# Sums of x in one run while GpSimd is held, sums of w_in moved, and chunk 4's transposes ahead of its v rows

## The chip, the cores and the metric

The kernel runs on one core of one Trainium2 chip. The metric is the device time of one execution in microseconds (us); lower is better. A core has five engines that run side by side, each in its own program order: TensorE (PE) multiplies matrices into PSUM, VectorE (DVE) and ScalarE (ACT) work elementwise on PSUM and SBUF, GpSimd (POOL) works elementwise on SBUF, and SyncE (SP) here only issues DMA transfers. They wait for each other on semaphores, which the framework places from the data dependences. The order of the instructions on each engine is the order in which the program calls them: there is no scheduler that changes it.

## The reference

Two layers follow each other. The first is a recurrent attention ("retention") over 768 steps, for 4 batches, 8 heads and a head size of 64:

```
gamma = 1.0 - 2.0 ** (-5.0 - arange(8));  scale = 1 / sqrt(64)
for t in range(768):
    state = gamma * state + outer(k[t], v[t])      # one 64 x 64 state for each batch and head
    y[t]  = scale * (q[t] @ state)
x = y, reordered to (3072 tokens, 512)
```

The second is a feed-forward layer: `h = x @ w_in` (512 to 2048), `g = gelu_tanh(h)`, `out = g @ w_out` (2048 to 512). Inputs and output are float32; the kernel computes in float16 with float32 sums.

## The kernel before

The sequence is cut into 6 chunks of 128 steps; a chunk has 4 batches, so 512 tokens. For each chunk c and batch b the kernel loads the rows of q, k and v, scales and casts them to float16, transposes q and k (by a DMA from chunk 2 on), forms the 128 x 128 scores of a head (`a_ps`, masked on DVE into `a_sb`), adds what the state contributes (`y_ps`), writes the result scaled by `dec` into `xT[c]`, and updates the state `st`.

The matrix products of the feed-forward layer go by quadrants with 7 block products in place of 8 (Winograd's form of Strassen's method). That needs sums of quadrants of both factors: `s_g` of g and `t_w` of w_out for the second product of every chunk, and `s_x` of x and `t_in` of w_in for the first product of chunks 3, 4 and 5 (the first product of chunks 0 to 2 is a plain one, `moe1` and `moe1_two`). The sums of x and w_in run on DVE, the sums of g mostly on POOL.

```python
s_x = const.tile([128, 4, 2, 2, 128], F16, name="s_x")

def tt(eng, out, in0, in1, op):
    eng.tensor_tensor(out=out, in0=in0, in1=in1, op=op)      # "L393" in the profile

def win_sums(i):          # 4 DVE sums of 128x512 float16 for one quarter of w_in
    ...
    tt(nc.vector, t[1], q[0, 1], q[1, 1], ALU.add)
    tt(nc.vector, t[2], t[1], q[0, 0], ALU.subtract)
    tt(nc.vector, t[3], q[0, 0], q[0, 1], ALU.subtract)
    tt(nc.vector, t[4], q[1, 0], t[2], ALU.subtract)

def x_sums(c, *keys):     # up to 4 DVE sums of 128x512 float16
    ...
    for j, in0, in1 in ops:
        if j in keys:
            tt(nc.vector, t[j], in0, in1, ALU.subtract)

def att_S(c, *bs):        # state update: products on PE (mm_s), 8 small instructions on DVE (ev_S)
    mm_s(c, bs)
    ev_S(c, bs)

def att_AY(c, bs, tag, ca, abs_, eng):   # outputs of chunk c, batches bs; scores of chunk ca, batches abs_
    for b in bs:   mm_yc(c, b, tag)
    for b in abs_: mm_A(ca, b)
    for b in bs:   mm_yi(c, b)
    if tag == "o":
        for b in abs_: ev_A(ca, b)
    for b in bs:   ev_Y(c, b, eng)
    if tag != "o":
        for b in abs_: ev_A(ca, b)

def prep_kT(c, b):        # cast of k on ACT, then the DMA transpose of q and k, issued from SP
    prep1(AC, "k", c, b)
    dma_T(c, b)

def run(units, after):    # unit i of the feed-forward layer on PE, then what is listed under i
    for i, u in enumerate(units):
        u()
        for f, *args in after.get(i, ()):
            f(*args)
```

The kernel is a row of such runs. The first runs the second product of chunk 0 (`units_0`, 15 units); the next the first product of chunk 1 (`moe1_two`, 16 units), then the second product of chunk 1 (`units_w(1)`, 14 units), the first product of chunk 2 (`moe1(2, fc)`, 16 units). The lists beside them are in the diff. From there on, `step(c)` for c = 2, 3, 4 mixes the second product of chunk c (units `u[0]` to `u[13]`), the first product of chunk n = c+1 (`h`, with the seven products `h.mm(0..6)`) and the attention of chunk m = c+2:

```python
for i in range(2):
    G = (2 * i, 2 * i + 1)
    for g in G:
        h.mm(0, g); h.keep(AC, 0, g)     # keep: ACT copies a PSUM bank to SBUF
        h.mm(1, g); h.add(1, g)          # add: DVE adds a PSUM bank to such a copy, which frees the bank
    h.act(1, *G)                         # act: gelu on ACT
    if i == 0: u[0](); u[1](); A(m, 0)   # A: scores on PE, masked on DVE
    else:      u[7](); u[8](); A(m, 2); sums(n, 0, 1, 2)    # sums: sums of g on POOL
    for g in G:
        h.mm(2, g); h.keep(AC, 2, g)
        h.mm(3, g); h.keep(AC, 3, g)     # mm(3) takes a bank that add(1) freed
    ...
    h.mm(4, *G); h.add(4, *G); h.act(4, *G)
    if i == 1:
        u[11](); sums(n, 0, 4); Y(m, 3)  # u[11] ends in a store of output rows, issued from POOL
    h.mm(5, *G); h.add(5, *G)
    if i == 0: u[4](); Y(m, 1); u[5](); St(m, 0, 1)
    elif m < NCk: x_sums(m, 1, 2); u[12]()
    h.mm(6, *G)
    ...
    if i == 0: u[6]()
    else:
        u[13](); St(m, 2, 3)
        if m < NCk: x_sums(m, 3, 4)
```

Of the kernel before, what the change touches and what calls it, by code (L numbers as in the profile page):

```python
# [16 lines left out]
def kernel(  # L17
# [417 lines left out]
    t_in = {}  # L435
    s_x = const.tile([128, 4, 2, 2, 128], F16, name="s_x")

# [16 lines left out]

    def x_sums(c, *keys):
        t = {j: s_x[:, j - 1] for j in (1, 2, 3, 4)}
        w = {(K, x): x_blk(c, K, x) for K in range(2) for x in range(2)}
        ops = (
            (1, w[0, 1], w[0, 0]),
            (2, w[1, 1], t[1]),  # L460
            (3, w[1, 1], w[0, 1]),
            (4, w[1, 0], t[2]),
        )
        for j, in0, in1 in ops:
            if j in keys:
                tt(nc.vector, t[j], in0, in1, ALU.subtract)

# [90 lines left out]
    class Half:  # L558
# [10 lines left out]
        def rhs(self, key, k):  # L569
            if key in s_g:  # L570
                return s_x[:, key - 1, k]
            return x_blk(self.c, *key)[:, k]
# [260 lines left out]
    def rows_of(c):  # L833
        for b in range(B):
# [14 lines left out]
            11: [(mm_Y, 0, "h"), (att_T, 2, AC), (ev_Y, 1, 0)],  # L849
            12: [(mm_Y, 1, "att"), (ev_Y, 1, 1), (mm_s, 1, (0,))],  # L850
            13: [(att_1A, 2), (ev_S, 1, (0,))],
            14: [(att_S, 1, 1)],
        },
# [9 lines left out]
        {  # L863
            0: [(att_T, 3)],
            1: [(mm_Y, 2, "o"), (ev_Y, 1, 2)],
            2: [(att_1A, 3)],
            3: [(att_S, 1, 2), (g_sums, PO, 1, 0, 4, 0, 1)],
            4: [(prep1, AC, "q", 2, 0)],
            5: [(mm_Y, 3, "o"), (ev_Y, 1, 3), (prep_kT, 2, 0)],
            6: [(att_S, 1, 3), (prep1, AC, "q", 2, 1)],  # L870
            7: [(g_sums, PO, 1, 4, 8, 0, 1), (prep_kT, 2, 1)],
# [3 lines left out]
            11: [(g_sums, PO, 1, 0, 4, 1, 2), (prep_kT, 2, 3), (rows_of, 3)],  # L875
            13: [(win_sums, 0)],
            14: [(att_AY, 1, (), "o", 2, (0, 1), None), (prep1, PO, "v", 2, 0), (prep1, PO, "v", 2, 1)],
# [6 lines left out]
            4: [(att_AY, 2, (0, 1), "h", 2, (2, 3), AC)],  # L884
            1: [(win_sums, 1)],
            6: [(prep_qk, 3, 0)],
            7: [(att_S, 2, 0, 1), (prep_qk, 3, 1)],
            9: [(att_AY, 2, (2, 3), "h", 2, (), AC), (att_S, 2, 2, 3), (prep_qk, 3, 2)],
            10: [(prep1, PO, "v", 3, b) for b in range(B)],
            11: [(prep_qk, 3, 3), (rows_of, 4)],  # L890
            13: [(win_sums, 2)],
        },
# [3 lines left out]
    def sums(c, f, *keys, eng=PO):  # L896
        for f0 in range(f, f + 4, 2):
# [5 lines left out]
            0: [(win_sums, 3)],  # L903
            2: [(att_AY, 3, (), "att", 3, (0, 1), None)],
            3: [(g_sums, PO, 2, 0, 2)],
            6: [(att_AY, 3, (0, 1), "o", 3, (2, 3), VE)],
            7: [(g_sums, PO, 2, 2, 4), (prep1, PO, "v", 4, 0), (prep1, PO, "v", 4, 1)],
            8: [(att_S, 3, 0, 1), (prep_qk, 4, 0)],
            11: [(g_sums, PO, 2, 4, 6), (prep_qk, 4, 1), (rows, 5, 0), (rows, 5, 1)],
            12: [(att_AY, 3, (2, 3), "o", 3, (), VE), (att_S, 3, 2, 3)],  # L910
            14: [(x_sums, 3, 1, 2, 3, 4)],
            15: [(g_sums, PO, 2, 6, 8), (prep1, PO, "v", 4, 2), (prep1, PO, "v", 4, 3)],
        },
# [26 lines left out]
    def step(c):  # L940
# [8 lines left out]
        for i in range(2):  # L949
# [44 lines left out]
            if i == 1:  # L994
                u[11]()
                sums(n, 0, 4)
                Y(m, 3)
            h.mm(5, *G)
# [6 lines left out]
            elif m < NCk:  # L1005
                x_sums(m, 1, 2)
                u[12]()
# [8 lines left out]
            if i == 0:  # L1016
                u[6]()
            else:
                u[13]()
                St(m, 2, 3)  # L1020
                if m < NCk:
                    x_sums(m, 3, 4)

# [40 lines left out]
```

## Time and profile before

| | us |
|---|---|
| time, median of 3 runs | 211.17 (210.99 to 212.71) |
| span of the profiled execution | 207.6 |
| PE busy | 193.7 (93% of the span) |
| DVE busy | 148.9 (72%) |
| POOL busy | 133.5 (64%) |
| ACT busy | 117.8 (57%) |

The span is the time from the first to the last instruction in the trace of one execution. "Busy" is the time in which an engine had an instruction under way. Lines such as L393 name the line of the program that issued an instruction; because `tt` is a helper, all sums have the line L393, and the tile they write tells them apart: `s_x` and `t_in` (DVE), `s_g` (POOL), `h_sb` and `o_sb` (DVE additions of a PSUM bank). L581 is a matrix product of `h.mm`, L499 one of `u[...]`, L350 one of the plain first product, L208 the scores, L267 and L286 the state update on PE and DVE, L198 the DMA transpose, L86 a load of rows. Some rows of the table of groups (busy us, mean ns of one, then the idle time before them and what ended most of it):

```profile
L221 DVE TENSOR_TENSOR a_sb<-a_ps,mask 128x512 f16<-128x512 f32 x48 | 30.5, 683 | 10.2 <-PE a_ps L208 8.1
L393 DVE TENSOR_TENSOR h_sb<-h_ps,h_sb 128x512 f32<-128x512 f32 x36 | 22.9, 683 | 7.9 <-ACT h_sb L143 7.2
L286 DVE SCALAR_TENSOR_TENSOR st<-st,cst,s_ps 64x128 f16<-64x128 f16 (+1 forms) x80 | 20.6, 319 | 0.7 <-PE s_ps L267 0.5
```

Times within the span are given below as "at 139.9", in us from its start.

### The profile page before, as it was taken

The page shows a single profiled execution, that of the slowest core. Times are in us where ns is not written, and L with a number is a line of the kernel's source. Part 1 is how long each engine was busy: PE and PEld are TensorE (multiplying, and loading weights), DVE is VectorE, ACT ScalarE, POOL GpSimd, SP SyncE. Part 2 cuts the span into 40 slices and gives each one's busy share as a digit, 9 for nine tenths or more (in the row PEclk, how much of TensorE's full clock was granted, in tenths as well). Part 3 has the DMA queues.
Part 4 walks back from the last instruction along what each step waited for, and adds up shares of the span by engine and source line. Part 5 has one row for each costly group of instructions (what it writes and reads, how often), then busy time and mean ns, then how long its engine had stood idle before and what let it go on. Part 6 is the DMA issues. An engine that isn't in the chain of part 4 may idle for free.

```text
span 207.6 us, 5024 instructions
## 1 busy us (share of the span) xinstructions
PE 193.7 (93%) x2012; PEld 149.9 (72%) x2012; DVE 148.9 (72%) x295; ACT 117.8 (57%) x216; POOL 133.5 (64%) x132
## 2 busy tenths in 40 slices
PE   5798999999999989999979999994999999999993
PEld 1456747788687868654567888874788888888882
DVE  5346669679978999969796966998844883336720
ACT  2384564463399318356638697444876285876321
POOL 0599333952099999558399739479919479598200
PEclk9999999999999999999999999999999999999998
DMA  7999999999967998999999596520250031002204
GB/s 167 288 257 207 206 206 277 346 296 275 288 153 104 213 250 185 181 280 244 213 215 207 122 255 151 179 107 2 67 37 0 3 163 43 0 0 99 106 14 188
DMA packets 87094, 34.24 MB, mean 165 GB/s; under 512 B 80032, under 2 KB 84512, under 8 KB 87072
## 3 DMA queue, kind: packets, MB, share of 16 engines
q1 hardware_dynamic: 73920, 19.25, 43.7%
q0 software_dynamic: 6624, 12.58, 23.4%
q10 hardware_dynamic: 6528, 2.10, 4.0%
q8 instruction: 15, 0.25, 0.5%
q14 instruction: 7, 0.06, 0.1%
HBM read 27.63 MB, written 6.29 MB: 163 GB/s over the span
## 4 chain that ended last, share of the span: by engine, by line
PE 75%; DVE 12%; POOL 3%; DMA 3%; ACT 2%; SPq 2%; issue 1%; DVEq 0%; ACTq 0%
PE o_ps L499 27%; PE h_ps L350 17%; PE h_ps L581 15%; DVE s_x L393 5%; DVE st L286 4%; PE o_ps L619 3%; DMA k<-in_k_dram 3%; PE y_ps L243 3%; PE a_ps L208 3%; PE o_ps L652 2%; PE y_ps L230 2%; DVE h_sb L393 2%; POOL qk L159 2%; ACT g L370 1%; SPq L86 1%
## 5 line engine op out<-in xcount | busy, mean ns | idle before, releaser
L350 PE MATMUL h_ps<-xT,w_in 128*128 128x256 f16 (+2 forms) x296 | 45.6, 304 | 0.5 <-ACT g L370 0.5
L370 ACT ACTIVATE g<-h_ps 128x512 f16<-128x512 f32 (+1 forms) x54 | 31.1, 583 | 21.9 <-PE h_ps L350 20.2
L393 POOL TENSOR_TENSOR s_g<-g 128x512 f16<-128x512 f16 x30 | 35.3, 1185 | 12.6 <-ACT g L370 8.2
L221 DVE TENSOR_TENSOR a_sb<-a_ps,mask 128x512 f16<-128x512 f32 x48 | 30.5, 683 | 10.2 <-PE a_ps L208 8.1
L350 PEld LDWEIGHTS <-w_in 128*128 128x128 f16 x296 | 26.5, 98 | 15.2 <-issue 1.2
L370 ACT ACTIVATE g<-h_sb 128x512 f16<-128x512 f32 x36 | 21.8, 632 | 22.8 <-DVE h_sb L393 22.7
L499 PEld LDWEIGHTS <-s_g 128*128 128x128 f16 x320 | 30.7, 98 | 5.0 <-POOL s_g L393 1.0
L499 PE MATMUL o_ps<-t_w,s_g 128*128 128x256 f16 x240 | 29.4, 273 | 0.8 <-POOL s_g L393 0.8
L393 DVE TENSOR_TENSOR h_sb<-h_ps,h_sb 128x512 f32<-128x512 f32 x36 | 22.9, 683 | 7.9 <-ACT h_sb L143 7.2
L159 POOL TENSOR_TENSOR v<-v,cst 128x512 f16<-128x512 f32 x20 | 21.0, 1071 | 7.2 <-DMA v<-in_v_dram 4.5
L581 PEld LDWEIGHTS <-t_in 128*128 128x128 f16 x192 | 18.0, 98 | 6.4 <-issue 3.5
L499 PEld LDWEIGHTS <-g 128*128 128x128 f16 x208 | 20.2, 98 | 2.5
L393 POOL TENSOR_TENSOR s_g<-s_g,g 128x512 f16<-128x512 f16 x18 | 21.0, 1168 | 1.4
L286 DVE SCALAR_TENSOR_TENSOR st<-st,cst,s_ps 64x128 f16<-64x128 f16 (+1 forms) x80 | 20.6, 319 | 0.7 <-PE s_ps L267 0.5
L581 PE MATMUL h_ps<-s_x,t_in 128*128 128x256 f16 x144 | 18.1, 273 | 3.1 <-DVE h_sb L393 3.0
L393 POOL TENSOR_TENSOR s_g<-g,s_g 128x512 f16<-128x512 f16 x18 | 20.8, 1168 | 0.1
L143 ACT COPY h_sb<-h_ps 128x512 f32<-128x512 f32 x36 | 19.2, 599 | 1.5 <-PE h_ps L581 1.3
L499 PE MATMUL o_ps<-w_out,g 128*128 128x256 f16 x160 | 19.1, 273 | 0.0
L259 DVE TENSOR_TENSOR xT<-y_ps,dec 128x512 f16<-128x512 f32 x20 | 13.3, 683 | 4.1 <-PE y_ps L243 4.1
L581 PEld LDWEIGHTS <-w_in 128*128 128x128 f16 x144 | 13.9, 98 | 1.9
L143 ACT CAST qk<-q 128x512 f16<-128x512 f32 x20 | 12.6, 630 | 2.2 <-DMA q<-in_q_dram 2.2
L143 ACT CAST qk<-k 128x512 f16<-128x512 f32 x20 | 12.6, 631 | 0.1
(81 smaller groups left out, 279.0 us busy)
## 6 DMA issues: line engine op xcount, KB each, us to landing
out_dram<-o_sb POOLq DMA_DIRECT2D x10, 512.0 KB, 3.1
k<-in_k_dram SPq DMA_DIRECT2D x18, 256.0 KB, 4.6
q<-in_q_dram SPq DMA_DIRECT2D x18, 256.0 KB, 4.7
v<-in_v_dram SPq DMA_DIRECT2D x18, 256.0 KB, 4.7
w_in<-in_moe_w_in_dram POOLq DMA_DIRECT2D x4, 512.0 KB, 9.0
w_out<-in_moe_w_out_dram POOLq DMA_DIRECT2D x4, 512.0 KB, 14.1
q<-in_q_dram POOLq DMA_DIRECT2D x4, 256.0 KB, 11.2
k<-in_k_dram POOLq DMA_DIRECT2D x4, 256.0 KB, 9.5
```

The source lines that it names most:

```text
L143: eng.copy(out=out, in_=in_)
L159: eng.tensor_tensor(out=t, in0=src, in1=cst[:, col:col + H].unsqueeze(2).broadcast_to([128, H, Dh]), op=ALU.mult,)
L208: nc.tensor.matmul(out=ps[j][:, hp], lhsT=t[j * 64:(j + 1) * 64, 1, hp], rhs=t[j * 64:(j + 1) * 64, 0, hp], start=True, stop=True,)
L221: nc.vector.tensor_tensor(out=s, in0=ps[j], in1=mask[:, j], op=ALU.mult)
L243: nc.tensor.matmul(out=y_ps[j * 64:(j + 1) * 64, hp], lhsT=h16["v", c, b][:, 2 * hp + j], rhs=a_sb[c, b, j][:, hp], start=(c == 0), stop=True,
L259: nc.vector.tensor_tensor(out=x, in0=ps, in1=dec, op=ALU.mult)
L286: nc.vector.scalar_tensor_tensor(out=t[:, :, hp], in0=t[:, :, hp], scalar=cst[sl, OG + hp:OG + hp + 1], in1=s_ps[sl, :, hp], op0=ALU.mult, ...
L350: nc.tensor.matmul(out=out, lhsT=w_in_sb[wi][:, kc, wr * 128:(wr + 1) * 128], rhs=xT[c][:, kc, t0:t1], start=(kc == 0), stop=(kc == NHP - ...
L370: nc.scalar.activation(out=out, in_=in_, func=AF.Gelu_apprx_tanh, scale=1.0)
L393: eng.tensor_tensor(out=out, in0=in0, in1=in1, op=op)
L499: nc.tensor.matmul(out=po, lhsT=lhs(c, lk, fp, a), rhs=rhs(rk, fp), start=(new and fp == 0 and (last or a == 0)), stop=(stop and fp == NP ...
L581: nc.tensor.matmul(out=self.ps[G, k][:, p], lhsT=self.lhs(lk, 2 * G + p, kc), rhs=self.rhs(rk, kc), start=(new and p == 0 and kc == 0), st ...
```

## The change

The change moves instructions and adds three tiny ones; no arithmetic of the result is changed. Parts 1 and 2 are for keeping DVE's float16 sums apart in time from POOL's work, part 3 for fewer DVE instructions, part 4 for having the transposed q and k of chunk 4 earlier and for a more even load of ACT. The parts:

1. `x_sums` is no longer split in two halves around the state update: the four sums of x stand in one run on DVE, right behind the last part of `xT` that they need. Behind them stands `hold`: a copy of one element of the last sum, on POOL. As POOL works in program order and the copy has to wait for the last sum, nothing that follows on POOL can start before the four sums are done. The fourth sum gets a second buffer (by the chunk's parity), because its old value is still being read at the new place.
2. `win_sums(0)` moves from the end of the run of `moe1_two(1, ...)` to its beginning, where POOL is idle, and `win_sums(1)` from the beginning of the run of `units_w(1)` to its end, beside `win_sums(2)` and `win_sums(3)`.
3. Two pairs of state updates of chunk 1, of one batch each, are merged into updates of two batches: `att_S(1, 0, 1)` and `att_S(1, 2, 3)`. The copy of the transposed q and k of chunk 1, batch 3, moves from DVE to ACT.
4. In the run of `moe1(2, ...)` the attention of chunk 3 moves back by one to three units; the casts of q and k of chunk 4, batches 0 and 1, stand one behind each of the units 6 to 9 in place of two behind 8 and two behind 11; the loads of the v rows of chunk 4 are issued behind the transposes of its batches 0 and 1 in place of ahead of them; and the casts of v of chunk 4 come two ahead and two behind of the last sums of g of chunk 2.

```diff
@@ -433,7 +433,10 @@
 
 
     t_in = {}
-    s_x = const.tile([128, 4, 2, 2, 128], F16, name="s_x")
+    s_x = const.tile([128, 5, 2, 2, 128], F16, name="s_x")
+
+    def sx(c, j):
+        return s_x[:, j - 1 + (j == 4 and c % 2)]
 
     def win_sums(i):
         h, p0 = i // 2, i % 2 * 2
@@ -452,8 +455,8 @@
         x = xT[c].rearrange("p (K k) (a b t) -> p K b k a t", K=2, a=2, b=2)
         return x[:, K, 1 - col]
 
-    def x_sums(c, *keys):
-        t = {j: s_x[:, j - 1] for j in (1, 2, 3, 4)}
+    def x_sums(c):
+        t = {j: sx(c, j) for j in (1, 2, 3, 4)}
         w = {(K, x): x_blk(c, K, x) for K in range(2) for x in range(2)}
         ops = (
             (1, w[0, 1], w[0, 0]),
@@ -462,8 +465,10 @@
             (4, w[1, 0], t[2]),
         )
         for j, in0, in1 in ops:
-            if j in keys:
-                tt(nc.vector, t[j], in0, in1, ALU.subtract)
+            tt(nc.vector, t[j], in0, in1, ALU.subtract)
+
+    def hold(c):
+        nc.gpsimd.tensor_copy(out=misc[0:1, 1:2], in_=sx(c, 4)[0:1, 0, 0, 0:1])
 
     PROD = (
         ("X", (0, 0), (0, 0), True, False),
@@ -568,7 +573,7 @@
 
         def rhs(self, key, k):
             if key in s_g:
-                return s_x[:, key - 1, k]
+                return sx(self.c, key)[:, k]
             return x_blk(self.c, *key)[:, k]
 
         def mm(self, n, *Gs):
@@ -847,9 +852,9 @@
             8: [(att_T, 1), (preps, 1, 2)],
             10: [(att_1A, 1), (preps, 1, 3)],
             11: [(mm_Y, 0, "h"), (att_T, 2, AC), (ev_Y, 1, 0)],
-            12: [(mm_Y, 1, "att"), (ev_Y, 1, 1), (mm_s, 1, (0,))],
-            13: [(att_1A, 2), (ev_S, 1, (0,))],
-            14: [(att_S, 1, 1)],
+            12: [(mm_Y, 1, "att"), (ev_Y, 1, 1)],
+            13: [(att_1A, 2)],
+            14: [(att_S, 1, 0, 1)],
         },
     )
 
@@ -861,19 +866,18 @@
             for fp in range(NF // 2)
         ],
         {
-            0: [(att_T, 3)],
+            0: [(att_T, 3, AC)],
             1: [(mm_Y, 2, "o"), (ev_Y, 1, 2)],
-            2: [(att_1A, 3)],
-            3: [(att_S, 1, 2), (g_sums, PO, 1, 0, 4, 0, 1)],
+            2: [(att_1A, 3), (win_sums, 0)],
+            3: [(g_sums, PO, 1, 0, 4, 0, 1)],
             4: [(prep1, AC, "q", 2, 0)],
             5: [(mm_Y, 3, "o"), (ev_Y, 1, 3), (prep_kT, 2, 0)],
-            6: [(att_S, 1, 3), (prep1, AC, "q", 2, 1)],
+            6: [(att_S, 1, 2, 3), (prep1, AC, "q", 2, 1)],
             7: [(g_sums, PO, 1, 4, 8, 0, 1), (prep_kT, 2, 1)],
             8: [(prep1, AC, "q", 2, 2)],
             9: [(prep_kT, 2, 2)],
             10: [(prep1, AC, "q", 2, 3)],
             11: [(g_sums, PO, 1, 0, 4, 1, 2), (prep_kT, 2, 3), (rows_of, 3)],
-            13: [(win_sums, 0)],
             14: [(att_AY, 1, (), "o", 2, (0, 1), None), (prep1, PO, "v", 2, 0), (prep1, PO, "v", 2, 1)],
             15: [(g_sums, PO, 1, 4, 8, 1, 2), (prep1, PO, "v", 2, 2), (prep1, PO, "v", 2, 3)],
         },
@@ -882,13 +886,12 @@
         units_w(1),
         {
             4: [(att_AY, 2, (0, 1), "h", 2, (2, 3), AC)],
-            1: [(win_sums, 1)],
             6: [(prep_qk, 3, 0)],
             7: [(att_S, 2, 0, 1), (prep_qk, 3, 1)],
             9: [(att_AY, 2, (2, 3), "h", 2, (), AC), (att_S, 2, 2, 3), (prep_qk, 3, 2)],
             10: [(prep1, PO, "v", 3, b) for b in range(B)],
-            11: [(prep_qk, 3, 3), (rows_of, 4)],
-            13: [(win_sums, 2)],
+            11: [(prep_qk, 3, 3)] + [(rows, 4, b) for b in range(B)],
+            13: [(win_sums, 1), (win_sums, 2)],
         },
     )
 
@@ -901,15 +904,16 @@
         [(lambda fc=fc: moe1(2, fc)) for fc in range(NF)],
         {
             0: [(win_sums, 3)],
-            2: [(att_AY, 3, (), "att", 3, (0, 1), None)],
             3: [(g_sums, PO, 2, 0, 2)],
-            6: [(att_AY, 3, (0, 1), "o", 3, (2, 3), VE)],
-            7: [(g_sums, PO, 2, 2, 4), (prep1, PO, "v", 4, 0), (prep1, PO, "v", 4, 1)],
-            8: [(att_S, 3, 0, 1), (prep_qk, 4, 0)],
-            11: [(g_sums, PO, 2, 4, 6), (prep_qk, 4, 1), (rows, 5, 0), (rows, 5, 1)],
-            12: [(att_AY, 3, (2, 3), "o", 3, (), VE), (att_S, 3, 2, 3)],
-            14: [(x_sums, 3, 1, 2, 3, 4)],
-            15: [(g_sums, PO, 2, 6, 8), (prep1, PO, "v", 4, 2), (prep1, PO, "v", 4, 3)],
+            4: [(att_AY, 3, (), "att", 3, (0, 1), None)],
+            6: [(prep1, AC, "q", 4, 0)],
+            7: [(g_sums, PO, 2, 2, 4), (prep_kT, 4, 0)],
+            8: [(prep1, AC, "q", 4, 1)],
+            9: [(att_AY, 3, (0, 1), "o", 3, (2, 3), VE), (prep_kT, 4, 1), (vrows, 4), (rows, 5, 0), (rows, 5, 1)],
+            11: [(att_S, 3, 0, 1), (g_sums, PO, 2, 4, 6)],
+            12: [(att_AY, 3, (2, 3), "o", 3, (), VE), (x_sums, 3), (hold, 3)],
+            13: [(att_S, 3, 2, 3)],
+            15: [(prep1, PO, "v", 4, 0), (prep1, PO, "v", 4, 1), (g_sums, PO, 2, 6, 8), (prep1, PO, "v", 4, 2), (prep1, PO, "v", 4, 3)],
         },
     )
 
@@ -993,8 +997,11 @@
             h.act(4, *G)
             if i == 1:
                 u[11]()
+                Y(m, 3)
+                if m < NCk:
+                    x_sums(m)
+                    hold(m)
                 sums(n, 0, 4)
-                Y(m, 3)
             h.mm(5, *G)
             h.add(5, *G)
             if i == 0:
@@ -1003,7 +1010,6 @@
                 u[5]()
                 St(m, 0, 1)
             elif m < NCk:
-                x_sums(m, 1, 2)
                 u[12]()
             h.mm(6, *G)
             if m == NCk and i == 1:
@@ -1018,8 +1024,6 @@
             else:
                 u[13]()
                 St(m, 2, 3)
-                if m < NCk:
-                    x_sums(m, 3, 4)
 
     for c in range(2, NCk - 1):
         step(c)
```

Set out by engine: PE has the same instructions in a slightly different order; DVE has 16 state-update instructions of two batches in place of 32 of one batch, and one copy less; ACT has one copy more; POOL has three one-element copies more.

## Prediction

> **What bounds the kernel now.** I read the times by engine first, then the table of stretches, then PE's waits, then the chain of waits, and last the time order of DVE and POOL at the places that the chain names. PE is busy 93% of the span, so only its standstills can be won, and the table of stretches says where they are (columns: stretch, its length, then for each engine busy us and number of instructions, then PE's clock, DMA share, GB/s):
>
> ```profile
> 68.00:86.00 18.00, 17.25 (x221) 14.73 (x220) 17.88 (x35) 6.89 (x14) 16.44 (x15) 1.00 1.05 211
> 86.00:104.00 18.00, 17.94 (x177) 9.41 (x176) 14.71 (x37) 11.13 (x20) 10.54 (x10) 1.00 1.02 240
> 104.00:112.00 8.00, 6.51 (x64) 5.37 (x63) 7.53 (x10) 3.73 (x7) 7.89 (x7) 1.00 1.02 209
> 112.00:130.00 18.00, 18.00 (x209) 14.83 (x207) 12.71 (x25) 14.53 (x28) 12.56 (x12) 1.00 0.80 182
> 130.00:143.00 13.00, 9.97 (x114) 8.23 (x112) 12.89 (x21) 4.96 (x10) 9.25 (x9) 1.00 0.32 109
> 143.00:204.00 61.00, 61.00 (x595) 53.43 (x595) 34.63 (x59) 37.98 (x73) 37.95 (x36) 1.00 0.18 51
> ```
>
> The reader is to see that PE stands 3.0 us in 130 to 143, 1.5 in 104 to 112, 0.75 in 68 to 86, and not at all after 143: nothing that the change does in chunk 5 can bring time. The DMA share is 1 up to 112. PE's waits (us in total, times, longest) name the causes:
>
> ```profile
> PE h_ps L581 <- DVE h_sb L393: 3.0, 1, 3.0
> ...
> PE a_ps L208 <- DMA qkT<-qk: 1.4, 1, 1.4
> ...
> PE o_ps L499 <- POOL s_g L393: 0.8, 1, 0.8
> PE a_ps L208 <- DVE qkT L145: 0.5, 1, 0.5
> ```
>
> Together 5.7 us: the pool to win from. The chain of waits (start, us, what) shows the largest as a queue on DVE without a pause:
>
> ```profile
> 132.75 1.20 DVE h_sb L393 x2
> 133.94 1.85 DVE s_x L393
> 135.82 0.42 DVE s_x L393
> 136.24 1.02 DVE st L286 x4
> ...
> 138.48 3.67 DVE s_x L393 x2
> ...
> 142.19 0.70 DVE h_sb L393
> ```
>
> The addition into `h_sb` at 142.19 is the `h.add(1)` that frees a bank for `h.mm(3)`; PE was ready at 139.9. In this queue one sum takes 0.42 us and others 1.85, though all are 128x512 float16. In the time order of DVE the same is seen in the sums of w_in, with POOL at work and with POOL waiting or only issuing stores:
>
> ```profile
> 61.61 1.28 DVE L393 TENSOR_TENSOR t_in<-w_in 128x512 f16<-128x512 f16 x1
> 62.93 1.26 DVE L393 TENSOR_TENSOR t_in<-t_in,w_in 128x512 f16<-128x512 f16 x1
> ...
> 87.14 0.42 DVE L393 TENSOR_TENSOR t_in<-w_in 128x512 f16<-128x512 f16 x1
> 87.47 0.42 DVE L393 TENSOR_TENSOR t_in<-w_in,t_in 128x512 f16<-128x512 f16 x1
> ```
>
> The second kind starts every 0.33 us or so. The eight in a row from 86.35 to 89.28 cost 0.366 each.
>
> [...] 0.42 against 1.3 us, and POOL's sums of g grow from 1.15 to 1.33 us beside them. [...] `h_sb`, `a_sb` and `xT`, with one input in PSUM, stay at 0.68 us beside POOL here. [...] rows issued at 88.21 land 6.4 us later here (the DMA answer for that moment).
>
> **The change part by part.** (a) *State updates and copy, chunk 1.* 16 instructions of one batch took 3.53 us; 8 of two batches take 2.29 (both in DVE's time order). With the 0.69 us copy gone to ACT as well, PE's scores at 54.5 no longer wait for DVE. ACT then copies in 1.01 us, behind one gelu, from about 51.7 to 52.7; PE wants it at 54.0. Gain: the wait, 0.5.
>
> (b) *Sums of w_in.* `win_sums(0)` goes to about 55.6, where POOL waits until 56.6 for gelu; the first ones take 0.35, the rest still collide, and DVE has room there. `win_sums(1)` leaves 70.3 to 75.2. POOL's sums of g, 1.22 to 1.34 us there against 1.15, and its casts, 2.41 a pair against 2.04, lose about 0.5 + 0.2 + 0.4 + 0.3 = 1.4 us of collisions in four groups, so the `s_g` for which PE waits at 76.2 comes about 1.9 earlier with part (a), and PE arrives 0.5 earlier. Gain: the wait, 0.75. The twelve sums at 86 take 12 x 0.366 = 4.4 us, beside POOL's stores; the last two or three meet the sums of g. DVE has 2 us of idle time just behind, so nothing is on the path.
>
> (c) *Chunk 4's transposes.* They are issued 4.4 us earlier (what the four v loads took from 99.50), so PE's wait at 107.45 to 108.88 falls: gain 1.4, and 0.2 more as `h.add(1)` of that step comes earlier. But the casts move from behind units 8 and 11 to behind units 6 to 9, and q of batch 0 lands at 88.21 + 6.4 = 94.6. Unit 6 ends at 85.5 + 7 x 0.87 + 0.55 (scores) = 92.2, its gelu at 92.8. ACT, in order, stands at the cast until 94.6; then cast 0.5 and the gelu of unit 7, 0.55, end at 95.7. Unit 9 needs the bank of unit 7 and would start at 85.5 + 9 x 0.87 + 0.55 = 93.9. That is a new wait of PE of about 1.8 us, if loads and PE come forward by the same amount. POOL casts the v that a load waits for earlier, and the DMA share is 0.74 at 80 to 82, so I take it that they do, nearly. Sum of (c): 1.6 - 1.8, about -0.1 +- 1.
>
> (d) *Sums of x.* For chunk 4 the DVE queue held 1.85 + 0.42 + 3.67 = 5.9 us of sums. In one run with POOL held: 4 x 0.36 = 1.45. The addition at 142.19 comes 4.5 earlier, at 137.7, before PE is ready at 139.9. Gain: all of the 3.0. `h.add(5)` comes 1.45 later, with its gelu and bank, for which PE has room until `h.mm(1)` of the next step. POOL stands from the store to the end of the sums, about 1.4 us, of which it had waited 0.8 or so anyway; its next consumer on PE is several us away. For chunk 3 the sums shrink from 4.8 us to 1.5 to 3, which is part of the 0.2 in (c). For chunk 5 nothing waits. Three copies of one element: the one that the kernel already has took 0.21 us; off the path.
>
> Sum: 0.5 + 0.75 - 0.1 + 3.0 = 4.15, and 0.2 for smaller waits in the same places: 4.35. 211.17 - 4.35 = 206.8.
>
> **The rivals.** *The loads gate.* If the rows of chunk 4 do not come forward with PE, because the DMA engines are full from 68 on and only the 0.5 of (a) reaches the SP queue by way of ACT's casts, (c) becomes -0.9, and 207.6 results. For it speaks a share of 1.02; against it the gap at 80 to 82. *The loads land sooner.* If the stores of chunk 1, which share the DMA engines at 87 to 92, are through earlier, the new wait may be half or nothing, (c) is up to +1.6 and the time 205.2. *The hold is late.* For chunk 3 the one-element copy stands behind a group of four sums of g which, by my count, run until the sums of x begin; if they run later, the sums of x take 1.3 each, and DVE, on which scores, state and sums are now packed closer, holds up `h.mm(0)` or `h.mm(3)` by 1 to 2 us: 208 to 209. *The DVE queue was not the only limit at 143.* If a copy on ACT or a transpose is not there at 139.9, part of the 3.0 stays. ACT's queue looks free from 137.5 on (`h_sb` copies end there), so I give it little.
>
> **Range and chances.** The first two waits and the fourth add up to 4.25 and look sure within 0.4; the spread comes from (c), -1 to +1.6, and from the packed DVE, 0 to -1.5. I take 205.2 to 209.0. The 2% mark lies at 206.95, a gain of 4.2, close to my middle: faster 0.54, same 0.43, slower 0.03.
>
> **What would show it.** (a) and (b): no wait of the scores for `qkT` on DVE, no wait for `s_g` at 75. (c): a wait of ACT's cast for the load of q and k of chunk 4 at 91 to 97, a wait of L350 for gelu behind it, and none of the scores for the transpose. (d): all sums of x of chunk 4 at 0.42, POOL idle beside them, no wait of L581 for `h_sb` at the start of the last step but one. I am wrong if ACT never waits for those rows, if the sums of x stay over 1 us, or if a new wait of over 1 us shows behind 112.

## The result, and the profile after

| | us | ratio to before |
|---|---|---|
| kernel before, 4 runs in turn with the changed one | 211.86 (210.99 to 212.71) | |
| changed kernel, 4 runs | 205.80 (205.25 to 206.25) | 0.9713 [0.9657, 0.9769] |
| changed kernel, measured again as a control of the experiments | 205.36 | 0.9722 [0.9694, 0.9751] |

The brackets hold 95% intervals. The change makes the kernel about 2.9% faster, some 6 us.

The table of stretches of the changed kernel (columns as before: stretch, length, then busy us and instructions of PE, PE's weight loads, DVE, ACT and POOL, then PE's clock, DMA share, GB/s). From 84 on its stretches are those of before, laid 2 us earlier:

```profile
84.00:102.00 18.00, 16.75 (x160) 8.92 (x158) 14.21 (x33) 10.30 (x18) 13.96 (x13) 1.00 1.17 243
102.00:110.00 8.00, 8.00 (x81) 5.72 (x79) 7.85 (x22) 4.04 (x8) 6.41 (x8) 1.00 1.00 224
...
128.00:141.00 13.00, 13.00 (x148) 11.01 (x143) 11.19 (x24) 8.62 (x17) 8.76 (x10) 1.00 0.38 123
```

PE is busy throughout where it had stood 3.0 us (128 to 141) and 1.5 us (102 to 110), and from 68 to 84 as well (16.00 of 16 us); 1.25 us have appeared in 84 to 102, where there had been next to none. PE's waits in the changed kernel from 40 to 200 us (us in total, times, longest):

```profile
PE h_ps L350 <- ACT g L370: 1.1, 1, 1.1
PE o_ps L657 <- ACT s_p L635: 0.2, 1, 0.2
PE y_ps L230 <- DVE xT L259: 0.2, 1, 0.2
```

None of the four waits of before is left. The new one is explained by the chain of waits of the changed kernel (start, us, what):

```profile
87.05 6.36 DMA q<-in_q_dram
...
93.43 0.62 ACT qk L143
94.05 0.51 ACT g L370
...
94.59 1.02 PE h_ps L350 x4
```

A load of q is under way for 6.36 us; ACT's cast `qk` stands in front of a gelu and waits for it; PE's block product needs the bank that this gelu empties. And the queue on DVE that had been the largest wait, in DVE's time order of the changed kernel (start, us, instruction):

```profile
131.97 0.42 DVE L393 TENSOR_TENSOR s_x<-xT 128x512 f16<-128x512 f16 x1
...
133.11 0.42 DVE L393 TENSOR_TENSOR s_x<-xT,s_x 128x512 f16<-128x512 f16 x1
133.44 1.28 DVE L393 TENSOR_TENSOR h_sb<-h_ps,h_sb 128x512 f32<-128x512 f32 x2
134.66 2.30 DVE L286 SCALAR_TENSOR_TENSOR st<-st,cst,s_ps 64x128 f16<-64x128 f16 x8
136.99 1.29 DVE L393 TENSOR_TENSOR h_sb<-h_ps,h_sb 128x512 f32<-128x512 f32 x2
```

The four sums of x, of which the first and the last are shown, take 0.42 or 0.43 each and 1.47 us together, from the first start to the next instruction, in place of 5.9. In the kernel before, POOL had been at work beside them, with sums of g and casts of v:

```profile
133.22 2.27 POOL L393 TENSOR_TENSOR s_g<-g,s_g 128x512 f16<-128x512 f16 x2
...
137.42 2.05 POOL L159 TENSOR_TENSOR v<-v,cst 128x512 f16<-128x512 f32 x2
```

The last line on DVE in the changed kernel holds the `h.add(1)` that frees the bank; PE, at about 138.9 here, finds it free. On POOL, in the changed kernel, the store's issue stands beside the first sums and the hold behind the last:

```profile
131.64 0.75 POOL L537 DMA_DIRECT2D out_dram<-o_sb  x1 [2.77 <-DVE o_sb L393]
133.60 0.17 POOL L471 CAST misc<-s_x 1x1 f32<-1x1 f16 x1 [1.21 <-DVE s_x L393]
```

The bracket is POOL's idle time before the instruction. It stood 1.21 us for the hold, and PE never noticed.

**Where the time went.** PE does the same work in both kernels, so the distance between two of its landmarks is what a part of the program cost. Means of two traces of each kernel; the two agree within 0.33 us in every part of before and within 0.06 in the changed one:

| from, to | before | changed | gain |
|---|---|---|---|
| run of `moe1_two`, chunk 1: part (a) | 18.75 | 17.98 | 0.77 |
| run of `units_w(1)`: part (b) | 16.68 | 15.92 | 0.76 |
| run of `moe1(2)`: the new wait | 18.43 | 19.88 | -1.45 |
| start of step 2 to the product of `s_x` (`h.mm(2)`): part (c) | 5.50 | 3.92 | 1.58 |
| from there to the last scores of step 3: part (d) | 37.43 | 34.12 | 3.31 |
| from there to the last product | 57.54 | 57.54 | 0.0 |
| sum | 154.33 | 149.35 | 4.98 |

The sum in the traces is 5.0; the runs give about 6. The traced executions of before are short ones: spans of 207.6 and 208.2, where its timed executions mostly have 208.4 to 210.7. The last section returns to this 1 us. The new wait and the wait for the transpose depend on when loads and transposes land, and that differs between executions: the new wait was 1.1 to 1.7 us in four traces with the same program up to there, and the wait for the transpose 0 to 1.6 us in four others, likewise.

### The profile page after: what moved, and what is told of

The parts are those of the page before. It is cut to its first block, busy times and chain, and to the rows that moved or that the text cites. A ratio compares the mean times of both kernels' runs of the same rounds, so it can differ in the third digit from the quotient of the medians.

```text
span 203.6 us, 5010 instructions
## 1 busy us (share of the span) xinstructions
PE 193.3 (95%) x2012; PEld 150.0 (74%) x2012; DVE 133.1 (65%) x278; ACT 119.0 (58%) x217; POOL 132.7 (65%) x135
## 4 chain that ended last, share of the span: by engine, by line
PE 85%; DMA 5%; ACT 3%; DVE 3%; issue 1%; SPq 1%; ACTq 0%; DVEq 0%
PE o_ps L504 31%; PE h_ps L586 19%; PE h_ps L350 16%; PE y_ps L243 4%; PE a_ps L208 4%; PE o_ps L624 3%; DMA q<-in_q_dram 3%; PE o_ps L657 3%; PE y_ps L230 2%; DMA iden<-rr_ident 2%; PE qkT_ps L188 2%; PE s_ps L267 1%; DVE a_sb L221 1%; ACT g L370 1%; ACT qkT L143 1%
## 5 line engine op out<-in xcount | busy, mean ns | idle before, releaser
L159 POOL TENSOR_TENSOR v<-v,cst 128x512 f16<-128x512 f32 x20 | 20.4, 1042 | 3.7 <-PE o_ps L657 2.6
L286 DVE SCALAR_TENSOR_TENSOR st<-st,cst,s_ps 64x128 f16<-64x128 f16 x64 | 18.2, 346 | 0.2
L393 POOL TENSOR_TENSOR s_g<-g,g_odd 128x512 f16<-128x512 f16 x6 | 6.9, 1154 | 9.8 <-ACT h_sb L143 9.8
## 6 DMA issues: line engine op xcount, KB each, us to landing
q<-in_q_dram POOLq DMA_DIRECT2D x4, 256.0 KB, 11.3
```

The costliest lines, as they stand in the source:

```text
L159: eng.tensor_tensor(out=t, in0=src, in1=cst[:, col:col + H].unsqueeze(2).broadcast_to([128, H, Dh]), op=ALU.mult,)
L286: nc.vector.scalar_tensor_tensor(out=t[:, :, hp], in0=t[:, :, hp], scalar=cst[sl, OG + hp:OG + hp + 1], in1=s_ps[sl, :, hp], op0=ALU.mult, ...
```

## The experiments

Ratios are to the kernel before, run in turn on the same chip. "In the trace" is the distance from the first block product of chunk 1 to the last product: 154.3 before, 149.35 in the changed kernel. In most diffs `-` is the changed kernel; where it is the kernel before, it is said.

**The changed kernel again**, unedited, as the control:

> The changed kernel once more, beside the variants. Expected: 0.971 of the kernel before, as measured, so about 205.8 us. If the span of the profiled execution is right about where time went (4.9 us from the first block product of chunk 1 to the end), a second measurement should lie nearer to 0.975 than to 0.966.

Measured: 205.36 us, 0.9722 [0.9694, 0.9751], in the trace 149.40. The first result stands, and so do its waits (1.2 us for gelu in place of 1.1).

### What the hold is worth

**Without the hold.** The one-element copies behind the sums of x are taken out, for chunks 3, 4 and 5; all else stays.

```diff
-  12: [(att_AY, 3, (2, 3), "o", 3, (), VE), (x_sums, 3), (hold, 3)],
+  12: [(att_AY, 3, (2, 3), "o", 3, (), VE), (x_sums, 3)],
...
       x_sums(m)
-      hold(m)
       sums(n, 0, 4)
```

> The changed kernel without the three one-element copies on POOL. My theory: the one run of sums, placed ahead of h.add(5), is what brings the 3.2 us, and the hold only makes the sums short. Without it POOL's two sums of g (2.3 us) follow the store at about 132.4, the four sums of x of chunk 4 take 2.5 to 4 us in place of 1.6, and h.add(1), which ended at 137.7 with PE ready at 138.9, comes 1 to 2.4 us later: a PE wait of 0 to 1.2, time +0 to +1.2 us. The rival, that the hold is the change: the sums go back to about 6 us, the PE wait to 2 or 3 us, time +2 to +3.

Measured: ratio 0.9875 [0.9826, 0.9925], so 1.5% or about 3.2 us of the gain are gone; 154.37 in the trace, 5.0 more than with the hold. The trace shows more than the runs: its execution has a span of 208.0, the other three that the ratio rests on have 205.4 to 206.3. The time is that of the rival or worse, but not by its reason, as the sums did not go back to 6 us. DVE in the kernel without hold:

```profile
133.36 3.00 DVE L393 TENSOR_TENSOR s_x<-xT 128x512 f16<-128x512 f16 x1
...
137.41 1.28 DVE L393 TENSOR_TENSOR h_sb<-h_ps,h_sb 128x512 f32<-128x512 f32 x2
```

and POOL at that moment:

```profile
133.80 2.27 POOL L393 TENSOR_TENSOR s_g<-g,s_g 128x512 f16<-128x512 f16 x2
```

The first sum of x takes 3.00 us, until both of POOL's sums are done, and the three behind it 0.42 or 0.43 each. With 4.05 us the sums are about as long as I had reckoned; what I had overlooked is who stands behind them. PE's waits:

```profile
PE h_ps L350 <- ACT g L370: 1.7, 1, 1.7
PE a_ps L208 <- DVE st L286: 1.2, 1, 1.2
PE o_ps L504 <- ACT g L370: 1.2, 2, 1.0
PE h_ps L586 <- DVE h_sb L393: 0.7, 1, 0.7
```

The first is the new wait of the changed kernel, 0.55 us longer in this execution; it lies ahead of the first place from which the hold was taken. The others stand in three different chunks. At 109.7 (chunk 3, whose last two sums took 1.27 and 1.26 beside POOL's casts of v) PE waits for the state updates behind the sums; at 138.2 (chunk 4) for a bank that a late `h.add` frees; at 169.6 (chunk 5, where the first sum again took 3.00) for the gelu behind a late `h.add(5)`. Since the one run stands ahead of `h.add(5)`, its length reaches PE there, where the split sums of before had not. By the landmarks of the table, the hold was worth 1.45, 1.42 and 1.56 us in these three chunks of this trace. Of the gain of 3.31 in part (d), 1.9 us stayed without it: the one run alone had shortened the sums of chunk 4 from 5.9 to 4.05 us.

**A pause on POOL in place of the hold.** As above, but a one-element copy that has to wait for the first of POOL's two sums stands between them. It asks whether DVE's first sum then ends with the first of POOL's two.

```diff
-      sums(n, 0, 4)
+      for f0 in (0, 2):
+          g_sums(PO, n, f0, f0 + 2, keys=(4,))
+          if f0 == 0 and m < NCk:
+              nc.gpsimd.tensor_copy(out=misc[0:1, 1:2], in_=s_g[4][0:1, 1, 1, 127:128])
```

> The kernel without the hold, and with a copy of one element on POOL between the two sums of g that follow the store, which has to wait for the first of them. In the run without the hold the first sum of x took 3.0 us, as long as both of POOL's sums. My theory: [...] the sum then ends with the first of POOL's two: about 1.6 to 1.9 us, and one later sum takes about 1.2. The rival, that DVE just waits until POOL is idle for long, or that the 3.0 us have another cause: still 3 us.

Measured: 208.51 us, 0.9855 [0.982, 0.9891]. DVE:

```profile
132.07 1.90 DVE L393 TENSOR_TENSOR s_x<-xT 128x512 f16<-128x512 f16 x1
134.00 1.40 DVE L393 TENSOR_TENSOR s_x<-xT,s_x 128x512 f16<-128x512 f16 x1
```

and POOL:

```profile
132.51 1.17 POOL L393 TENSOR_TENSOR s_g<-g,s_g 128x512 f16<-128x512 f16 x1
133.74 0.27 POOL L1006 CAST misc<-s_g 1x1 f32<-1x1 f16 x1
133.97 1.14 POOL L393 TENSOR_TENSOR s_g<-g,s_g 128x512 f16<-128x512 f16 x1
```

The first sum now ends in POOL's pause, at 133.97, and the second behind POOL's second sum (it took 1.40, a little more than the 1.2 expected). As expected: here, where POOL's two sums otherwise follow each other without a gap, a wait of POOL's own between them brought the first sum from 3.00 to 1.90 us. The pause does not bring the time back, as the sums together still take 3.92 us (132.07 to 135.99).

**The kernel before, with nothing changed but the sums of x of the steps**: one run with the hold, as in the changed kernel, but the sums of chunk 3 (in the run of `moe1(2)`) as before. `-` is before; the second buffer and `hold`, which are those of the change, are left out of this diff and the next.

```diff
   if i == 1:
       u[11]()
-      sums(n, 0, 4)
       Y(m, 3)
+      if m < NCk:
+          x_sums(m, 1, 2, 3, 4)
+          hold(m)
+      sums(n, 0, 4)
...
-      x_sums(m, 1, 2)
       u[12]()
...
-      if m < NCk:
-          x_sums(m, 3, 4)
```

> The kernel before with the sums of x of chunks 4 and 5 in one run with the hold, in the steps only; nothing else changed. My theory: PE's wait of 3.0 us at 139.9 is the only one that goes: 211.1 - 3.0 to 3.3 = 207.8 to 208.1, ratio 0.984 to 0.986, with the other waits (0.5, 0.8, 1.4) as before. The rival, that the parts need each other: 1.5 us or less won here.

Measured: 207.37 us, 0.9806 [0.9778, 0.9834], somewhat better than expected; 3.05 less than before in the trace. The 3.0 us at 139.9 are gone, as the step said. It shows something about the other waits as well: the wait for the transpose did not occur, and in its place PE stood at 108.5, somewhat longer, for DVE:

```profile
PE h_ps L587 <- DVE h_sb L393: 1.8, 1, 1.8
```

Chunk 3's sums of x, 1.15 to 1.37 each beside POOL, put off the `h.add(1)` of step 2 to 109.5. The transpose and this DVE queue are two limits that end within a few tenths of each other, so earlier transposes alone won nearly nothing here: to win all of the 1.6 of part (c), the DVE queue has to be shorter too. Nothing that was edited stands ahead of this place. The transposes were issued 0.76 us ahead of the first product of step 2 in this trace, and 0.21 and 0.86 us behind it in the two of before: the wait for them, 1.4 and 1.6 us there, is partly a matter of the execution.

**The kernel before, sums split at their old places, POOL held behind each half**: is it the place or the quiet that counts? `-` is before.

```diff
   u[11]()
-  sums(n, 0, 4)
   Y(m, 3)
+  if m >= NCk:
+      sums(n, 0, 4)
...
   x_sums(m, 1, 2)
+  hold(m, 2)
+  sums(n, 0, 4)
   u[12]()
...
       x_sums(m, 3, 4)
+      hold(m, 4)
```

> The kernel before with its sums of x in two halves at their old places, POOL held behind each half (the second copy of one element behind x_sums(3, 4), POOL's last sums of g of the step behind the first half). If quiet on POOL is what counts, the sums take 0.42 us each, the DVE queue at 133 to 142 shrinks by about 4.5 us as in the one run, and the time is 207.8 to 208.2. If the place ahead of h.add(5) and of the state update counts, or if holding POOL twice delays the sums of g, 209.5 or more.

Measured: 206.84 us, 0.9796 [0.9764, 0.9829], no slower than the one run and below what I expected. All four sums of chunk 4 take 0.41 to 0.43 at their old places, and the 3.0 us are gone. The first of each half:

```profile
133.84 0.41 DVE L393 TENSOR_TENSOR s_x<-xT 128x512 f16<-128x512 f16 x1
...
137.77 0.43 DVE L393 TENSOR_TENSOR s_x<-xT 128x512 f16<-128x512 f16 x1
```

The quiet on POOL is what counts; moving the sums together is not needed for it. In the trace this kernel is 3.64 us ahead of before, 0.58 more than the one run. That lies in chunk 3, which is the same in both: PE stood there 0.4 us for the transpose and 0.8 for `h_sb`, in place of 1.8. In chunk 5 the last sum still took 2.64, and PE waited for nothing.

### The new wait, and part (c)

**Later casts.** The casts of q and k of chunk 4 go behind units 8 to 11 in place of 6 to 9, by when the rows are to have landed.

```diff
-  6: [(prep1, AC, "q", 4, 0)],
-  7: [(g_sums, PO, 2, 2, 4), (prep_kT, 4, 0)],
-  8: [(prep1, AC, "q", 4, 1)],
-  9: [(att_AY, 3, (0, 1), "o", 3, (2, 3), VE), (prep_kT, 4, 1), (vrows, 4), (rows, 5, 0), (rows, 5, 1)],
-  11: [(att_S, 3, 0, 1), (g_sums, PO, 2, 4, 6)],
+  7: [(g_sums, PO, 2, 2, 4)],
+  8: [(prep1, AC, "q", 4, 0)],
+  9: [(att_AY, 3, (0, 1), "o", 3, (2, 3), VE), (prep_kT, 4, 0)],
+  10: [(prep1, AC, "q", 4, 1)],
+  11: [(att_S, 3, 0, 1), (g_sums, PO, 2, 4, 6), (prep_kT, 4, 1), (vrows, 4), (rows, 5, 0), (rows, 5, 1)],
```

> The changed kernel with the casts of chunk 4, batches 0 and 1, each two units of the run later (q behind 8, k and transpose behind 9, q behind 10, k and transpose behind 11, then the v loads). My theory: PE's 1.1 us wait of L350 for gelu at 93.5, which comes from ACT standing 1.0 us at the cast for the load of q, is the price of part 4. With the casts later both waits go and the step starts 1.1 to 1.5 us earlier: 204.3 to 204.8. The rival: DVE, which is packed from 97 to 108 there, sets the start of the step, and nothing or under 0.4 us is won.

Measured: 204.35 us, 0.9669 [0.9622, 0.9716]; in the trace 148.06, 1.3 less than the changed kernel. All that is left of PE's waits from 40 to 200:

```profile
PE o_ps L657 <- ACT s_p L635: 0.2, 1, 0.2
PE y_ps L230 <- DVE xT L259: 0.2, 1, 0.2
```

The wait for gelu was the whole price of part (c), and it came from the place of the casts in ACT's order: two units later the rows are there, and the transposes still come in time. The same kernel measured again:

> The kernel with the later casts of chunk 4 once more, beside the next one. Expected: 0.967 to 0.970 of before, about 204.4 to 205 us; PE without a wait of over 0.4 us from 40 to 200.

Measured: 0.9634 [0.9592, 0.9677], 148.07 in the trace. It is the fastest kernel of these experiments, together with the one with spread casts below.

**The run of `moe1(2)` as before.** Part 4 of the change undone; the sums of x of chunk 3 stay behind unit 14, without a hold.

```diff
-  11: [(prep_qk, 3, 3)] + [(rows, 4, b) for b in range(B)],
+  11: [(prep_qk, 3, 3), (rows_of, 4)],
...
-  6: [(prep1, AC, "q", 4, 0)],
-  7: [(g_sums, PO, 2, 2, 4), (prep_kT, 4, 0)],
...
+  7: [(g_sums, PO, 2, 2, 4), (prep1, PO, "v", 4, 0), (prep1, PO, "v", 4, 1)],
+  8: [(att_S, 3, 0, 1), (prep_qk, 4, 0)],
+  11: [(g_sums, PO, 2, 4, 6), (prep_qk, 4, 1), (rows, 5, 0), (rows, 5, 1)],
...
+  14: [(x_sums, 3)],
```

> The changed kernel with the run of the first product of chunk 2 listed as before (attention of chunk 3, casts, v loads ahead of the transposes, sums of x of chunk 3 behind unit 14 without a hold); all else as changed. My theory from the two traces: part 4 lost 1.6 us in the run and won 1.5 + 0.2 at the scores of chunk 4, net 0.1, so the time is within 0.5 us of the changed kernel. The rival: earlier transposes bring their 1.4 us in full, and this kernel is 1.4 us slower.

Measured: 205.73 us, 0.9726 [0.9686, 0.9765], the same as the changed kernel. The wait for the transpose is 0.2 in its trace, without any part (c), and a wait of 0.7 for `h_sb` stands beside it; of chunk 3's sums the first took 0.43, the other three 1.15 to 1.37. Against the changed kernel the run of `moe1(2)` is 1.55 us shorter, and from the start of step 2 to the last scores of step 3 it takes 1.16 more. So part 4 as written is worth nothing beside the other parts: what it wins behind, it loses in front. That the wait for the transpose is so short may be chance, as it was 0 and 0.4 in the two kernels above, whose program is that of before up to this place.

### Parts (a) and (b)

**Sums of w_in at their old places.**

```diff
-  2: [(att_1A, 3), (win_sums, 0)],
+  2: [(att_1A, 3)],
...
+  13: [(win_sums, 0)],
...
+  1: [(win_sums, 1)],
...
-  13: [(win_sums, 1), (win_sums, 2)],
+  13: [(win_sums, 2)],
```

> The changed kernel with win_sums(0) and win_sums(1) at their places of before. My theory: POOL's sums of g are 1.2 to 1.3 us again, PE's wait for s_g at 75 is back with 0.7 to 0.8 us, but ACT then reaches the cast for the load of q of chunk 4 later and its stand of 1.0 us shrinks by as much, so only part of it reaches the end: 205.4 + 0 to 0.75 us. The rival, that the moved sums of w_in are worth more than the wait that they remove: over 1 us slower.

Measured: ratio 0.9748 [0.9714, 0.9782], 150.24 in the trace, 0.9 more than the changed kernel. The times alone do not tell the two kernels apart (0.9722 with an interval that overlaps), the trace does: the wait for `s_g` is back with 0.8 us, which is part (b) by itself. I had left open that it is given back at the new wait; that stayed at 1.2, as q landed 8.68 us behind the start of the run, in place of 8.55: the load came later together with PE.

**State updates by single batches at their old places, the copy on DVE** (part 3 of the change undone):

```diff
-  12: [(mm_Y, 1, "att"), (ev_Y, 1, 1)],
-  13: [(att_1A, 2)],
-  14: [(att_S, 1, 0, 1)],
+  12: [(mm_Y, 1, "att"), (ev_Y, 1, 1), (mm_s, 1, (0,))],
+  13: [(att_1A, 2), (ev_S, 1, (0,))],
+  14: [(att_S, 1, 1)],
...
-  0: [(att_T, 3, AC)],
+  0: [(att_T, 3)],
...
-  3: [(g_sums, PO, 1, 0, 4, 0, 1)],
+  3: [(att_S, 1, 2), (g_sums, PO, 1, 0, 4, 0, 1)],
...
-  6: [(att_S, 1, 2, 3), (prep1, AC, "q", 2, 1)],
+  6: [(att_S, 1, 3), (prep1, AC, "q", 2, 1)],
```

> The changed kernel with part (a) undone: state updates of chunk 1 by single batches at their old places, and the copy of the transposed q and k of batch 3 on DVE. My theory: the scores' wait of 0.5 us for that copy is back, and with the state updates again ahead of it on DVE 0.3 us more, but the stand of ACT for the load of q of chunk 4 takes some of it back: 0 to 0.8 us slower, 205.4 to 206.2. The rival: nothing is lost, as later waits take up the slack.

Measured: 209.51 us, 0.9892 [0.9848, 0.9937]; 154.37 in the trace, 5.0 more than the changed kernel. The expectation failed by far. Two things were not in it. First, PE's waits have a new head:

```profile
PE h_ps L350 <- DVE xT L259: 2.3, 1, 2.3
PE h_ps L350 <- ACT g L370: 1.9, 1, 1.9
PE a_ps L208 <- DVE qkT L145: 0.5, 1, 0.5
```

With the single updates in place `win_sums(0)`, at its new place, has three of its four sums at 1.30 to 1.37 beside POOL, ends at 60.5, and a state update of 1.75 us still stands between it and the `xT` that PE needs next. (The second line is the new wait of the changed kernel, which is longer here.) Second, the stretches of that moment (columns as above; the last but two is PE's clock):

```profile
62.00:63.00 1.00, 0.03 (x1) 0.03 (x2) 0.97 (x3) 0.00 (x0) 0.92 (x2) 0.73 0.00 1
63.00:64.00 1.00, 1.00 (x5) 0.70 (x6) 0.99 (x6) 0.00 (x0) 1.00 (x2) 0.50 1.15 260
...
65.00:66.00 1.00, 1.00 (x7) 0.71 (x6) 0.00 (x0) 1.00 (x2) 1.00 (x1) 0.56 0.00 0
```

PE stands from 60.65 to 62.97, and its granted clock is halved from about 62.5 to 65.9. Some 3 us of products at half clock cost about another 1.5 us, an estimate from these clocks. 2.3 + 0.5 + 1.5 = 4.3 make up the 4.4 by which the run of `moe1_two` is longer in this trace than in the changed kernel; the rest of the 5.0 lies in the longer wait for gelu. So the lower clock came on top of the standstill in this execution; that the standstill brought it is not shown. It may not be so in each: one of the six kept a mean clock of 0.998, and its span is 206.0, where the other five have 207.1 to 208.5 with 0.981 to 0.992.

**Spread casts of chunk 2.** Beside the later casts of chunk 4, those of q and k of chunk 2 are spread from unit 2 on, so that ACT's casts stand further from each other.

```diff
-  2: [(att_1A, 3), (win_sums, 0)],
-  3: [(g_sums, PO, 1, 0, 4, 0, 1)],
-  4: [(prep1, AC, "q", 2, 0)],
-  5: [(mm_Y, 3, "o"), (ev_Y, 1, 3), (prep_kT, 2, 0)],
+  2: [(att_1A, 3), (win_sums, 0), (prep1, AC, "q", 2, 0)],
+  3: [(g_sums, PO, 1, 0, 4, 0, 1), (prep_kT, 2, 0)],
+  4: [(prep1, AC, "q", 2, 1)],
+  5: [(mm_Y, 3, "o"), (ev_Y, 1, 3), (prep_kT, 2, 1)],
...  (batches 2 and 3 behind units 7, 8 and 10, 11)
```

> The kernel with the later casts, and the eight casts of q and k of chunk 2 spread over units 2 to 11 of the run of moe1_two(1) with two units in between without a cast, in place of one behind each of units 4 to 11, where PE takes 7.72 us for 64 products that take 6.98 elsewhere, at the pace of ACT (a gelu and a cast, 1.0 us a unit). My theory: ACT's pace is then under PE's 0.87 us a unit on average, and 0.4 to 0.7 us is won. The rival: the stretch is not limited by ACT, or the transposes and with them the loads of chunk 3 start as late as before and give it back: within 0.2 us.

Measured: 0.9646 [0.96, 0.9692], 148.07 in the trace, the same as with the later casts alone. The run of `moe1_two` is 0.3 shorter, and 0.3 us of wait for `s_g` appear at 74.5: PE then comes before POOL. The rival's number holds, but neither of its reasons: ACT did limit the stretch, and the gain is given back at POOL's sums of g.

**The kernel before, traced again**, for its waits and for where its usual executions are longer:

> The kernel before, once more with its trace. Most of its times lie at 211 and more, while the execution behind the first profile took 209.5. If my account of the waits holds for a usual execution too, the four waits of PE (3.0, 1.4, 0.8, 0.5) are there again in the same places with about the same lengths, together 5.5 to 7 us behind 40 us, and the rest of the difference lies ahead of 40 us or in the clock. If a wait is much longer than in the first trace, the change wins more there than I counted.

Measured: span 208.2, the same four waits (3.0, 1.6, 0.8 and 0.5 us at the same places), and again one of its shorter executions. It confirms the waits and leaves the second question open.

## Why the prediction was right, step by step

- **What bounds the kernel.** Right: in the traces the gain lies in PE's four waits of before, less the new one, and behind chunk 4 the two kernels take the same 57.54 us.
- **(a), 0.5.** The wait is gone as said, ACT's copy took 52.55 to 53.56. The run gained 0.77; the 0.27 more belong to no single wait in the list. What the step did not see is that (a) and (b) lean on each other. At its new place `win_sums(0)` stands ahead of an `xT` that PE needs soon. With the old state updates it starts 6.17 us behind the start of the run in place of 5.49, three of its sums take 1.30 to 1.37 beside POOL in place of two (1.38 and 1.37), and one more state update of 1.75 us follows before that `xT`. With (b) in place and (a) undone, the loss is 3.6 us by the ratios (0.9892 against 0.9722), not 0.5.
- **(b), 0.75.** Measured 0.76. As foreseen, two sums of `win_sums(0)` took 0.42 and two still collided (1.38 and 1.37). Of the twelve sums at 86, the last one met POOL (1.38), so that they took 5.4 us and not 4.4; it is off the path.
- **(c), 1.6 - 1.8.** Right in the new wait, its place and its cause, and in the sum, near nothing. The gain behind was 1.58. The new wait was 1.1, and the run as a whole 1.45 longer, in place of 1.8: q landed at 93.4, 8.55 us behind the start of the run, where the rows issued at 88.21 in before had landed 9.06 behind it. Of the rivals here, "the loads gate" did not happen, and "the loads land sooner" did in a small part (from 86 to 93 in before, the stores' queue took 49.6% of the time of the 16 DMA engines and the queue of loads and transposes 52.0%). What the step left out: DVE's queue in chunk 3 ends at the same moment as the transpose, so the 1.6 need shorter sums of x there too; and the wait for the transpose is no fixed sum, but was 0 to 1.6 us in four traces whose program is the same up to there. That the sum of (c) came out so close is in part luck.
- **(d), 3.0.** Measured 3.31 in the changed kernel, 3.05 alone. The store's issue did not slow the sums beside it (0.42), and POOL's stand of 1.2 us was free. "For chunk 5 nothing waits" holds only with the hold: without it the kernel lost 1.6 us behind chunk 4.
- **"The hold is late".** It was not. In chunk 3 POOL's sums of g ended at 104.34 and the sums of x began at 104.24; all four took 0.42.
- **The size.** The terms give 4.35 (with 1.6 - 1.8 taken as -0.1, and 0.2 for smaller waits), the traces 4.98: (a) and (d) were 0.27 and 0.31 too small, the net of (c) 0.23 too low, and no separate 0.2 is to be found. The remaining 1 us between the traces and the runs is no step of mine; I had put the time of a usual execution and the waits of a short one side by side. The measured 205.80 lies near the lower end of the range, which was that wide for the sake of (c), but (c) is not what took it there: that the range still covers the result is luck.

## What to carry to other kernels

A VectorE sum of two float16 tensors of SBUF took 0.42 us here with GpSimd quiet and mostly 1.15 to 3.00 us beside GpSimd's sums and casts. So ask for each such sum what GpSimd does at that moment, and if the sum is on the path, hold GpSimd with a one-element copy that depends on the last of the run: three such copies of 0.17 us bought about 3 us here. When an order is changed to bring a transfer forward, put the first consumer on an in-order engine no earlier than the landing, or it stops the work queued behind it (a cast ahead of its load stood in front of a gelu, and PE waited 1.1 us here). And before a part is credited with its wait, look for the second limit that ends at the same moment: two of the four gains here needed another part to become real.

## What the runs showed of the hardware

- **How long a sum takes beside POOL.** With POOL held a sum of x took 0.42 us. Beside two of POOL's sums of g that stood without a gap (2.27 us for both) the first sum of x took 3.00 us, and 1.90 us once a dependent copy stood between the two. In both traces its record begins 0.44 us ahead of POOL's, more than it takes alone, and yet it came last; why is not shown. Elsewhere, as in the three sums of w_in of 1.30 to 1.37 beside four sums of g in the trace with (a) undone, each ended behind another one of POOL's without such a copy. In all these cases the record of the slow sum ended 0.28 or 0.29 us behind that of a POOL sum. What decides behind which one is not settled; in the trace without the hold, the wait was not over with one instruction of POOL. What makes a sum slow beside POOL is not shown by these runs either.
- **A store's issue did not slow a sum.** The sum that began at 131.97 took 0.42 us, inside a store's issue on POOL of 0.75 us that began at 131.64.
- **Half a clock, once behind a standstill.** In the trace with (a) undone the granted clock was halved for 3.4 us, from 1.8 us into a standstill of PE of 2.3 us. The standstill of 3.0 us in chunk 4 has no such stretch near it in either trace of before (1.00 from 130 to 143 in the first; 0.9 or more in every slice but the last in the second), nor has the 1.9 us for gelu in the trace with (a) undone itself (0.9 or more in every slice behind 68). The trace of the one run of sums in the kernel before, with 1.8 us at 108.5, has a mean clock of 0.998, which leaves about 0.8 us at half clock in all of it, by estimate. What decides is not settled.
- **The missing 1 us.** In the first trace of the changed kernel the clock is halved from 7.3 to 14.1 us, ahead of all that is compared here. Its mean clock is 0.983, and 6.8 x 0.5 / 203.6 = 0.017 is what that stretch takes from it. The timed executions of before show mean clocks of 0.973 to 0.992 nearly throughout; reckoned alike, an estimate, that is 3.3 to 11.3 us at half clock in a span of 209. The two traced ones have 0.997, and the changed kernel shows 1.0 in all six of its second measurement. Before's spans go with it: 207.7 us in its one timed execution with 1.0, 208.4 to 209.8 with 0.989 to 0.992, 209.3 to 211.2 with 0.973 to 0.983. That would account for the 1 us by which the runs gained more than the traces. It is argued, not shown: in the first trace of before the clock is 1.00 until the last product is done, in the second it is under 0.9 in the last slice alone, and where the lower clock stands in the timed executions is unknown.
